# Output stage of a three-part kernel: first two units in halves side by side, p's raw places exchanged, conversions in a set order

## The chip, the cores and the metric

The kernel runs on 1 core of one Trainium2 chip. The metric is the time of one execution in microseconds (us) of device time; of several runs the median counts. Lower is better.

## The reference

What is computed is a decayed causal attention and two feed-forward blocks behind it, all in float32:

```python
scores = scale * q @ k.T + (cum_i - cum_j), causal;  attn = softmax(scores);  x = attn @ v      # 4 batches, 8 heads, 576 x 64
h = x @ w_in;   g = max(0.01 * h, h);   x = g @ w_out         # 2304 tokens, 512 -> 2048 -> 512
a = x @ w_a;    b = x @ w_b;            out = (a * b) @ w_out2 # 2304 tokens, 512 -> 1536 -> 512
```

Only the last line is touched by the change, and of it the product with `w_out2` and the end of the two products before it.

## The kernel before

TensorE multiplies in a rounded float32 form. Each operand is split into a rounded part and the rest of it (high and low, function `parts`, L933 on ScalarE for the high part and L934 on VectorE for the low part), and each product is made in three passes (high x high, high x low, low x high). The matrices of the second feed-forward block are multiplied by a seven-product scheme on 2 x 2 blocks, so an operand of four blocks is first turned into seven (`seven_of_four`, L955 to L959): four blocks as they are, then three sums of them (L957 and L958 on VectorE), each set then split by `parts`.

**Third layer** (`l3_unit`, matmuls L1090). `a` and `b` are made for 6 pairs of 128-column blocks (i = 0 to 5), for token blocks u = 0 and u = 1 of 1024 tokens and a last one. `b`'s unit ends with the multiplication by `a` (L1103) and `p_store` (L1074 to L1076): two additions on VectorE and a store of p to DRAM. The very last of these, of i = 5 and u = 1, is put off (`held["store"]`) and called where the caller wants it.

**Fourth layer** (`l4_unit`, matmuls L1200). There are 9 units n of 2 x 128 tokens. A unit multiplies p by the six row blocks of `w_out2` (j = 0 to 5), 7 products of 3 passes for each j, 126 matmuls of 256 columns in all, into four banks of PSUM, and then adds the products up (L1207 to L1221) and stores the output rows. p comes back from DRAM in halves: half h = 0 holds j = 0 to 2 and half h = 1 holds j = 3 to 5 (`load_p`, DMA at L1172; `convert_p` makes the seven split blocks of a half). The weights come as four plus three blocks from DRAM (`load_o2`, DMA at L1149) and are split by `convert_o2`.

**Places.** SBUF is full, so raw and split operands land in places that the third layer has just done with. Raw p(0,1), the second half of unit 0, lands in a place that the third layer's operands for u = 0 leave; p(0,0) has a place of its own; p(1,0), p(1,1) and the later halves take turns in the four tiles of the third layer named o0, o1, a0, a1. Raw weight block 3 lands in two small tiles that are also used for other things (`words`); blocks 4 and 5 land in places that the third layer's operands for u = 1 leave.

**Order.** The kernel is written as a program order, and a scheduler decides the order of the instructions of each engine from it. The program before calls, between the steps of the third layer's last block (i = 5): after the first step the load and split of weight block 0, and the load of p(0,0); after the third step weight block 1; after the fourth step what is left of `later`, the load of p(0,1), the splits of p(0,0), weight block 2 and p(0,1), and the loads of weight block 3, p(1,0) and p(1,1). Then, behind the third layer, weight blocks 3 to 5, p(1,0) and p(1,1) are split, the put-off store is called, and the units follow one after the other, each with the loads and the split of unit n + 2 around it:

```python
    for n in range(NB1):
        if n + 2 < NB1:
            for h in range(2):
                load_p(n + 2, h)
        l4_unit(n)
```

Of the kernel before, what the change touches and what calls it, by code (L numbers as in the profile page):

```python
# [26 lines left out]
def kernel(  # L27
# [903 lines left out]

    def parts(hi, lo, src):
        nc.scalar.copy(hi, src)  # L933
        nc.vector.tensor_tensor(out=lo, in0=src, in1=f32(hi), op=ALU.subtract)  # L934
# [18 lines left out]
    def seven_of_four(w, t, op):  # L953

        parts(w(0)[:, 0:4], w(1)[:, 0:4], t)  # L955
        second = t[:, 1:2]
        nc.vector.tensor_tensor(out=t[:, 2:4], in0=t[:, 2:4], in1=second.to_broadcast([P, 2, *t.shape[2:]]), op=ALU.subtract)  # L957
        nc.vector.tensor_tensor(out=t[:, 1], in0=t[:, 1], in1=t[:, 0], op=op)  # L958
        parts(w(0)[:, 4:7], w(1)[:, 4:7], t[:, 1:4])  # L959

# [111 lines left out]
    def p_store(o, i, t0, n):  # L1072

        nc.vector.tensor_tensor(out=o[:, 1], in0=o[:, 1], in1=o[:, 3], op=ALU.add)  # L1074
        nc.vector.tensor_tensor(out=o[:, 1], in0=o[:, 1], in1=o[:, 0], op=ALU.subtract)
        nc.sync.dma_start(p_dram[i // 3, :, i % 3, :, t0 : t0 + n].rearrange("b p t -> p b t"), o)  # L1076

    def l3_unit(i, z, u):
# [22 lines left out]
        def store():  # L1101
            if z:
                nc.vector.tensor_tensor(out=o[:, 1:4], in0=o[:, 1:4], in1=at[:, 1:4], op=ALU.mult)  # L1103
                p_store(o, i, 512 * u, 512)

        def last():
            if (i, z, u) == (NP - 1, 1, 1):
                held["store"] = store
            else:
                store()  # L1110
# [40 lines left out]
    def convert_o2(i):  # L1151
        if i == 0:
            place = pools["ea"].tile([P, SLOT], F32R, tag="a", name=f"w_o2_{i}")
        elif i == 2:
            place = pools["ex"].tile([P, SLOT], F32R, tag="w", name=f"w_o2_{i}")
# [20 lines left out]
    def convert_p(n, h):  # L1176

        if n % 2 == 0 and h:
            x = pools["ex"].tile([P, 5384], F32R, tag="x", name=f"px_{n}")[:, 8:]
        else:  # L1180
            x = rounded(((8, None), (5 * SLOT + 72, 5384))[n % 2][h], 5376)
        x = xps[n, h] = x.rearrange("p (b l i t) -> p b l i t", b=7, l=2, i=3)
        seven_of_four(lambda l: x[:, :, l], raw_p[n, h], ALU.add)
# [3 lines left out]
    def l4_unit(n):  # L1187
# [4 lines left out]
        banks = [bank(f"o_{n}_{z}") for z in range(5 if final else 4)]  # L1192
# [3 lines left out]
        order = [(j, m) for m in PRODUCTS for j in range(NP)] if final else [(j, m) for j in range(NP) for m in PRODUCTS]  # L1196
        for j, m in order:
            z, y = place[m]
            for e, (xl_, wl) in enumerate(PASSES):
                nc.tensor.matmul(  # L1200
                    ps[m], xps[n, j // 3][:, X_ROWS[m], xl_, j % 3, :], wo2[j][:, O_COLS[m], wl, :],
                    start=(j == e == y == 0), stop=(j == NP - 1 and e == 2 and y == ends[z]),
                )
        o = words(F32, f"o_{n}").rearrange("p (b n) -> p b n", b=4)
# [127 lines left out]
    def y_pool():  # L1332
        e_ctx.close()
        pools["ey"] = e_ctx.enter_context(tc.tile_pool(name="ey", bufs=1))
# [32 lines left out]
    for i in range(NP):  # L1367
# [5 lines left out]
        for s, (z, u) in enumerate(steps):  # L1373
# [21 lines left out]
            if i == NP - 1:  # L1395
                if s == 0:
                    load_o2(0)
                    load_p(0, 0)
                    convert_o2(0)
                    load_o2(2)  # L1400
                if s == 2:
                    load_o2(1)
                    convert_o2(1)
                if s == 3:
                    while later:
                        later.pop(0)()
                    e_ctx.close()
                    pools["ex"] = e_ctx.enter_context(tc.tile_pool(name="ex", bufs=1))
# [12 lines left out]
    for h in range(2):  # L1421
        convert_p(1, h)
    held["store"]()
    for n in range(NB1):
# [3 lines left out]
        l4_unit(n)  # L1428
        if n + 2 < NB1:
            for h in range(2):  # L1430
                convert_p(n + 2, h)
# [30 lines left out]
```

## Time and profile before

| | |
|---|---|
| median of 3 runs | 1033.9 us (1032.48 to 1035.31) |
| the profiled execution, its time | 1030.66 us |
| its span, first to last instruction | 1028.9 us |
| TensorE busy | 1005.5 us (98%) |
| VectorE, ScalarE busy | 671.6 us (65%), 557.9 us (54%) |
| mean granted clock of TensorE | 0.992 |

The profile gives, for one execution, the busy time of each engine, the chain of work that ended last, the instructions in order of time, and for each wait what ended it. TensorE is busy nearly all the time, so a change can only win where TensorE stands still or runs at the lower clock. The fourth layer begins at about 877 us from the span's start.

### The profile page before, as it was taken

How to read it: one execution, taken by the hardware profiler on the slowest of the kernel's cores; microseconds unless marked ns; L12 is line 12 of the kernel's file. 1: busy time of each engine (PE TensorE's matmuls, PEld its weight loads, DVE VectorE, ACT ScalarE, POOL GpSimd, SP SyncE). 2: the span in 40 equal slices, each digit the busy share in tenths (PEclk: the TensorE clock that was granted, in tenths of full speed). 3: DMA queues.
4: the chain of work that ended last, by engine and by line, in shares of the span. 5: the costliest groups of instructions: out<-in, count | busy, mean ns of one | idle time of the engine just before them, and what ended most of it. 6: DMA issues, size and time to landing. Idle time of an engine off the chain costs nothing.

```text
span 1028.9 us, 19822 instructions
## 1 busy us (share of the span) xinstructions
PE 1005.5 (98%) x7299; PEld 913.8 (89%) x7299; DVE 671.6 (65%) x1383; ACT 557.9 (54%) x1144; POOL 178.4 (17%) x402
## 2 busy tenths in 40 slices
PE   6899999999999999999999999999999999899998
PEld 5677779999999999999999997888888888799998
DVE  5799656755626555264367547668686675898872
ACT  6688687986748867488455444232322222354430
POOL 3525325442413324133000000000000000000000
PEclk9899999999999999999999999999999999999999
DMA  8997145543532436321583123233151423757711
GB/s 218 270 266 217 48 96 110 106 93 62 112 78 62 92 62 110 80 55 45 188 298 119 62 62 103 94 122 118 57 164 41 159 100 125 238 150 203 212 53 42
DMA packets 230497, 125.78 MB, mean 122 GB/s; under 512 B 144704, under 2 KB 212160, under 8 KB 230400
## 3 DMA queue, kind: packets, MB, share of 16 engines
q1 hardware_dynamic: 224784, 118.67, 42.0%
q10 hardware_dynamic: 5616, 5.84, 1.7%
q8 instruction: 58, 0.95, 0.4%
q14 instruction: 39, 0.32, 0.1%
HBM read 95.29 MB, written 29.17 MB: 121 GB/s over the span
## 4 chain that ended last, share of the span: by engine, by line
PE 92%; DMA 4%; ACT 1%; DVE 1%; POOL 1%; issue 1%; SPq 0%; ACTq 0%; POOLq 0%; DVEq 0%
PE h L865 19%; PE y L895 19%; PE o L1200 12%; PE s L99 6%; PE b_b L1090 5%; PE b_a L1090 5%; PE av L99 5%; PE pp L99 4%; PE a_a L1090 3%; PE a_b L1090 3%; PE d_b L1090 3%; PE d_a L1090 3%; DMA homef<-in_moe_w_out_dram 2%; PE a_last L1122 2%; PE b_last L1122 2%; DMA homef<-o_dram 1%
## 5 line engine op out<-in xcount | busy, mean ns | idle before, releaser
L895 PE MATMUL y<-gh,homer 128*128 128x256 f32 x1152 | 227.2, 284 | 0.6 <-ACT gh L877 0.6
L865 PE MATMUL h<-xh,homer 128*128 128x256 f32 x1152 | 225.6, 283 | 0.9 <-ACT hs L878 0.9
L865 PEld LDWEIGHTS h<-xh,homer 128*128 128x128 f32 x1152 | 183.4, 188 | 5.6 <-issue 2.7
L895 PEld LDWEIGHTS y<-gh,homer 128*128 128x128 f32 x1152 | 183.8, 188 | 3.8 <-issue 2.1
L895 PE MATMUL y<-gl,homer 128*128 128x256 f32 x576 | 162.5, 284 | 0.0
L865 PE MATMUL h<-xl,homer 128*128 128x256 f32 x576 | 161.6, 281 | 0.0
L895 PEld LDWEIGHTS y<-gl,homer 128*128 128x128 f32 x576 | 108.4, 188 | 1.1 <-issue 0.9
L865 PEld LDWEIGHTS h<-xl,homer 128*128 128x128 f32 x576 | 108.3, 188 | 0.5
L390 POOL TENSOR_SCALAR p<-cumb,ncum_t 128x384 f32<-128x384 f32 (+2 forms) x112 | 75.7, 679 | 149.3 <-PE pp L99 86.3
L880 DVE TENSOR_TENSOR gl<-hs,gh 128x512 fp32r<-128x512 f32 x72 | 50.9, 707 | 71.9 <-ACT hs L878 71.3
L373 ACT ACTIVATE p<-p,stat 128x256 f32<-128x256 f32 (+3 forms) x123 | 73.6, 600 | 36.0 <-DVE stat L402 30.7
L402 DVE CUSTOM_DVE_ANT_0 p<-s,p 128x384 f32<-128x384 f32 (+2 forms) x100 | 48.4, 491 | 39.6 <-PE s L99 29.8
L877 ACT ACTIVATE gh<-h 128x512 fp32r<-128x512 f32 x72 | 42.7, 593 | 41.7 <-PE h L865 40.9
L411 ACT ACTIVATE p<-p,rec 128x384 f32<-128x384 f32 (+1 forms) x108 | 56.1, 572 | 11.5 <-DVE rec L379 10.6
L99 PE MATMUL pp<-ident,p 128*128 128x128 f32 (+1 forms) x376 | 62.2, 276 | 0.0
L1200 PE MATMUL o<-homer,homer 128*128 128x256 f32 x441 | 57.7, 284 | 0.0
L1200 PEld LDWEIGHTS o<-homer,homer 128*128 128x128 f32 x441 | 55.2, 191 | 0.2
L1200 PE MATMUL o<-w_o,homer 128*128 128x256 f32 x378 | 52.6, 284 | 1.4 <-ACT homer L933 1.4
L933 ACT CAST homer<-p 128x1536 fp32r<-128x1536 f32 (+1 forms) x26 | 33.7, 1320 | 35.3 <-DVE p L958 20.4
L1200 PEld LDWEIGHTS o<-w_o,homer 128*128 128x128 f32 x378 | 48.6, 191 | 2.1 <-ACT homer L933 1.8
L99 PEld LDWEIGHTS pp<-ident,p 128*128 128x128 f32 (+1 forms) x376 | 43.4, 139 | 4.0 <-issue 2.3
L99 PE MATMUL av<-pt,vn 128*64 128x320 f32 (+4 forms) x400 | 46.9, 372 | 0.0
(272 smaller groups left out, 2047.6 us busy)
## 6 DMA issues: line engine op xcount, KB each, us to landing
p<-p_dram SPq DMA_DIRECT2D x17, 768.0 KB, 6.6
p_dram<-p SPq DMA_DIRECT2D x12, 1024.0 KB, 4.3
cumb<-cum_dram SPq DMA_DIRECT2D x32, 288.0 KB, 3.9
homef<-in_moe_w_out_dram SPq DMA_DIRECT2D x15, 511.6 KB, 6.0
homef<-in_moe_w_in_dram SPq DMA_DIRECT2D x15, 510.5 KB, 4.7
raw_o<-in_moe_w_out_dram SPq DMA_DIRECT2D x12, 511.6 KB, 5.9
xq<-in_q_dram SPq DMA_DIRECT2D x144, 32.0 KB, 2.1
y_dram<-yo ACTq DMA_DIRECT2D x18, 256.0 KB, 2.9
```

The costliest lines, as they stand in the source:

```text
L99: return method(*args, **kw)
L373: act_att.activation(pt, pt, AF.Exp, bias=stat[:, 0, s : s + 1], scale=-1.0, accum_out=stat[:, 1, s : s + 1])
L390: made = pool_att.tensor_scalar(pt, cumb[:, :n], 1.0, ncum_t[:, t, bh : bh + 1], op0=ALU.mult, op1=ALU.add)
L402: dve_att.tensor_tensor_reduce(out=pt, in0=sp[:, :n], in1=pt, op0=ALU.add, op1=ALU.min, scale=1.0, scalar=ABOVE, accum_out=stat[:, 0, s : ...
L411: act_att.mul(ps[i], ps[i], rec[:, i : i + 1])
L865: made = nc.tensor.matmul(hps[:, u, :], w[:, c * P : c * P + P], x[:, c, :], start=(n == 0), stop=(n == 3 * ND - 1))
L877: nc.scalar.activation(gh, hps, AF.Prelu, alpha=0.01)
L880: nc.vector.tensor_tensor(out=gl, in0=hs, in1=f32(gh), op=ALU.subtract)
L895: nc.tensor.matmul(o, w[:, d * P : d * P + P], g[:, u, :], start=(fi == 0 and n == 0 and d % 2 == 0), stop=(fi == NF1 - 1 and n == 2 and d ...
L1090: nc.tensor.matmul(to, w[:, W_ROWS[m], wl, c2 * P : c2 * P + P], y[c2][xl_][:, Y_COLS[m], :], start=(first and c2 == e == 0), stop=(c2 == ...
L1122: nc.tensor.matmul(ps[:, f * T1 : f * T1 + T1], w[:, wb, wl, c2 * P : c2 * P + P], y[:, xb, xl_, c2 * T1 : c2 * T1 + T1], start=(f == m == ...
L1200: nc.tensor.matmul(ps[m], xps[n, j // 3][:, X_ROWS[m], xl_, j % 3, :], wo2[j][:, O_COLS[m], wl, :], start=(j == e == y == 0), stop=(j == N ...
```

## The change

Five edits, all around the start of the fourth layer:

- `l4_unit(n, h)` can do one half of a unit alone. Units 0 and 1 are now done as: first half of 0, first half of 1, second half of 0, second half of 1. All other units are as before.
- The raw places are exchanged: p(1,0) now lands where p(0,1) landed (the place left by u = 0), p(0,1) in o1, p(1,1) in a0, and the later halves take the four tiles in another rotation. The places of the split halves are exchanged in the same way.
- Raw weight block 3 lands in one piece of 1792 columns in a place that the third layer's last `a` weights leave, in place of the two small tiles; its split is then one instruction of each kind and not two.
- `seven_of_four` and `convert_o2` are made into generators, and `by_turns` names the order in which their pieces are called; `next_in` then adds an order dependence between each such instruction and the one before it on the same engine (ScalarE, VectorE), from the fourth step of i = 5 to the split of p(2,1). The put-off multiplication L1103 and store come between these pieces: the multiplication between weight blocks 4 and 5, the additions and the store within the split of unit 2.
- The split of unit 2 is called before the second half of unit 1.

```diff
+    border = {}
+
+    def next_in(engine, made):
+        if border:
+            if border.get(engine) is not None:
+                tc.add_manual_dep(made.ins, border[engine].ins.name, ORDER, reason="order between the stages")
+            border[engine] = made
+
     def parts(hi, lo, src):
-        nc.scalar.copy(hi, src)
-        nc.vector.tensor_tensor(out=lo, in0=src, in1=f32(hi), op=ALU.subtract)
+        next_in("act", nc.scalar.copy(hi, src))
+        next_in("dve", nc.vector.tensor_tensor(out=lo, in0=src, in1=f32(hi), op=ALU.subtract))
...
+        elif i == 3:
+            raw_o2[i] = [(plain(2 * SLOT, 7 * T1).rearrange("p (b n) -> p b n", b=7), 0, 7)]
...
+    def by_turns(turns, **of):
+        for name in turns.split():
+            next(of[name])
...
-        if (n, h) == (0, 1):
+        if (n, h) == (1, 0):
             src = plain(5392, 1536).rearrange("p (b i t) -> p b i t", b=4, i=3)
         else:
-            pool, tag = ("r", ("o1", "a0", "a1", "o0")[(2 * n + h - 2) % 4]) if n else ("ey", "s")
+            tag = {(0, 0): "s", (0, 1): "o1", (1, 1): "a0"}.get((n, h)) or ("a1", "o1", "a0", "o0")[(2 * n + h) % 4]
+            pool = "r" if n or h else "es"
...
-        if n % 2 == 0 and h:
-            x = pools["ex"].tile([P, 5384], F32R, tag="x", name=f"px_{n}")[:, 8:]
+        if n % 2 and h == 0:
+            x = pools["ex"].tile([P, 5440], F32R, tag="x", name=f"px_{n}")[:, 8:5384]
         else:
-            x = rounded(((8, None), (5 * SLOT + 72, 5384))[n % 2][h], 5376)
+            x = rounded(((8, 5 * SLOT + 72), (None, 5384))[n % 2][h], 5376)
...
-        order = [(j, m) for m in PRODUCTS for j in range(NP)] if final else [(j, m) for j in range(NP) for m in PRODUCTS]
+        js = range(NP) if h is None else range(3 * h, 3 * h + 3)
+        order = [(j, m) for m in PRODUCTS for j in js] if final else [(j, m) for j in js for m in PRODUCTS]
...
+                    load_p(1, 0)
+                    by_turns("a a b a b w b w", a=convert_p(0, 0), b=convert_p(1, 0), w=convert_o2(2))
                     load_p(0, 1)
-                    convert_p(0, 0)
-                    convert_o2(2)
-                    convert_p(0, 1)
-                    load_o2(3)
-                    load_p(1, 0)
-                    load_p(1, 1)
     later.pop(0)()
-    for j in range(4, NP):
+    for j in range(3, NP):
         load_o2(j)
-    for j in range(3, NP):
-        convert_o2(j)
-    for h in range(2):
-        convert_p(1, h)
-    held["store"]()
-    for n in range(NB1):
+    load_p(1, 1)
+    l4_unit(0, 0)
+    l4_unit(1, 0)
+    late_x = convert_p(1, 1)
+    by_turns(
+        "x x u x v s y w y y", x=convert_p(0, 1), y=late_x, s=held["store"], u=convert_o2(3), v=convert_o2(4), w=convert_o2(5)
+    )
+    l4_unit(0, 1)
+    for h in range(2):
+        load_p(2, h)
+    more = [convert_p(2, h) for h in range(2)]
+    by_turns("a a", a=more[0])
+    all_of(held["store"])
+    by_turns("a b b b", a=more[0], b=more[1])
+    border.clear()
+    for n in range(1, NB1):
...
-        l4_unit(n)
+        l4_unit(n, 1 if n < 2 else None)
```

On each engine the order of the instructions is the same up to these places, and the counts of matmuls are equal.

SyncE issues the DMAs. In its rows below, `p_dram<-p_0` is the store of p for i = 5, u = 0, the last that half 1 of the units 0 to 3 needs; `homef_1536` is the raw place left by u = 0, `p_0` and `p_1` on the left of an arrow are halves 0 and 1 of a unit, `t_o_3`, `homef_1792` and `homef_3584` are raw weight blocks. Before:

```order
L1076 DMA p_dram<-p_0_10896 128x4x512
L1172 DMA homef_1536_10964<-p_dram 128x12x128
L1172 DMA p_0_10989<-p_dram 128x12x128
L1172 DMA p_1_10991<-p_dram 128x12x128
L1149 DMA t_o_3_0_10985<-o_dram 128x1024
L1149 DMA homef_3584_11099<-o_dram 128x7x256
L1149 DMA t_o_3_4_10986<-o_dram 128x768
L1149 DMA homef_3584_11101<-o_dram 128x7x256
L1172 DMA p_0_11131<-p_dram 128x12x128
L1076 DMA p_dram<-p_1_11039 128x4x512
```

With the change, from the same place:

```order
L1196 DMA homef_1536_10971<-p_dram 128x12x128
L1092 DMA p_dram<-p_0_10899 128x4x512
L1167 DMA homef_1792_11100<-o_dram 128x1792
L1196 DMA p_1_10992<-p_dram 128x12x128
L1196 DMA p_1_11106<-p_dram 128x12x128
L1167 DMA homef_3584_11102<-o_dram 128x7x256
L1167 DMA homef_3584_11104<-o_dram 128x7x256
```

and, right behind these:

```order
L1196 DMA p_1_11338<-p_dram 128x12x128
L1196 DMA p_0_11336<-p_dram 128x12x128
L1196 DMA p_0_11355<-p_dram 128x12x128
L1255 DMA out_dram<-o_11328 128x512 x2
L1255 DMA out_dram<-o_11422 128x512
L1092 DMA p_dram<-p_1_11040 128x4x512
L1255 DMA out_dram<-o_11422 128x512
L1196 DMA p_0_11443<-p_dram 128x12x128
L1196 DMA p_1_11357<-p_dram 128x12x128
```

The load into `homef_1536`, now p(1,0), has moved ahead of the store; raw weight block 3 is one load and has moved ahead of p(0,1) and p(1,1); the loads of unit 2 (with one of unit 3, `p_0_11355`) stand behind all weights; the store of i = 5, u = 1 (`p_dram<-p_1`) has moved from behind one load of unit 2 to behind three loads of units 2 and 3 and three stores of output.

VectorE at the end of the third layer, from the last addition of `b` for u = 0 on (`a_1`, `p_1` belong to u = 1, `p_0` with a 768 or 384 wide row to the sums of p(0,0), `homer_5376` to its split). Before:

```order
L989 TENSOR_TENSOR p_0_10896<-b_b_0_10898,p_0_10896 128x512
L1103 TENSOR_TENSOR p_0_10896<-p_0_10896,a_0_10762 128x1536
L934 TENSOR_TENSOR homer_5376_10966<-p_0_10823,homer_5376_10966 128x4x384
L983 TENSOR_TENSOR a_1_10993<-b_a_1_10995,a_1_10993 128x512
L1074 TENSOR_TENSOR p_0_10896<-p_0_10896 128x512
L985 TENSOR_TENSOR a_1_10993<-d_a_1_10996,a_1_10993 128x512
L957 TENSOR_TENSOR p_0_10823<-p_0_10823 128x768
L977 TENSOR_TENSOR p_1_11039<-b_b_1_11041,p_1_11039 128x512
L1075 TENSOR_TENSOR p_0_10896<-p_0_10896 128x512
```

With the change:

```order
L1005 TENSOR_TENSOR p_0_10899<-b_b_0_10901,p_0_10899 128x512
L1119 TENSOR_TENSOR p_0_10899<-p_0_10899,a_0_10765 128x1536
L999 TENSOR_TENSOR a_1_10994<-b_a_1_10996,a_1_10994 128x512
L1090 TENSOR_TENSOR p_0_10899<-p_0_10899 128x512
L1001 TENSOR_TENSOR a_1_10994<-d_a_1_10997,a_1_10994 128x512
L1091 TENSOR_TENSOR p_0_10899<-p_0_10899 128x512
L947 TENSOR_TENSOR homer_5376_10973<-p_0_10826,homer_5376_10973 128x4x384
L993 TENSOR_TENSOR p_1_11040<-b_b_1_11042,p_1_11040 128x512
L995 TENSOR_TENSOR p_1_11040<-d_b_1_11043,p_1_11040 128x512
```

The two additions ahead of the store (L1074 and L1075, now L1090 and L1091) stand ahead of the split of p(0,0); the second was the eighth row behind the first row shown, and is now the fifth.

TensorE where the first half of unit 0 ends (`o_0_11135` to `o_3_11138` are unit 0's banks and `o_3_11293` is unit 1's; the operand on the right of a comma is the split p, `px_10978` p(0,1); `homer_3584_9374` is weight block 3). Before:

```order
L1200 MATMUL o_3_11138<-w_o_2_10973,homer_5376_10966 128x256 x2
L1200 MATMUL o_0_11135<-w_o_2_10973,homer_5376_10966 128x256 x5
L1200 MATMUL o_1_11136<-w_o_2_10973,homer_5376_10966 128x256 x5
L1200 MATMUL o_2_11137<-w_o_2_10973,homer_5376_10966 128x256 x5
L1200 MATMUL o_3_11293<-w_o_0_10825,homer_5376_11113 128x256 x2
L1200 MATMUL o_0_11290<-w_o_0_10825,homer_5376_11113 128x256 x2
L1200 MATMUL o_3_11138<-homer_3584_9374,px_10978 128x256
L1200 MATMUL o_0_11135<-homer_3584_9374,px_10978 128x256
L1200 MATMUL o_3_11293<-w_o_0_10825,homer_5376_11113 128x256
L1200 MATMUL o_0_11290<-w_o_0_10825,homer_5376_11113 128x256 x4
```

With the change (`o_0_11108` to `o_3_11111` are unit 0's, `o_0_11175` to `o_2_11177` unit 1's, `px_10974` is p(1,0), `homer_5376_11243` p(0,1), `homer_3584_9377` weight block 3):

```order
L1229 MATMUL o_1_11176<-homer_3584_10896,px_10974 128x256 x6
L1229 MATMUL o_2_11177<-homer_3584_10896,px_10974 128x256 x6
L1229 MATMUL o_0_11175<-w_o_2_10985,px_10974 128x256 x5
L1229 MATMUL o_1_11176<-w_o_2_10985,px_10974 128x256 x6
L1229 MATMUL o_2_11177<-w_o_2_10985,px_10974 128x256 x6
L1229 MATMUL o_3_11111<-homer_3584_9377,homer_5376_11243 128x256
L1229 MATMUL o_0_11108<-homer_3584_9377,homer_5376_11243 128x256
L1229 MATMUL o_1_11109<-homer_3584_9377,homer_5376_11243 128x256
L1229 MATMUL o_2_11110<-homer_3584_9377,homer_5376_11243 128x256
L1229 MATMUL o_3_11111<-homer_3584_9377,homer_5376_11243 128x256 x2
L1229 MATMUL o_0_11108<-homer_3584_9377,homer_5376_11243 128x256 x5
```

Before, the first matmuls on weight block 3 and p(0,1) stand behind the 63 matmuls of unit 0's first half and 4 of unit 1's; with the change they stand behind all 126 of both first halves.

## Rows read from the trace of the kernel before

**Rows 1.** The chain that ended last, from 850 us: start us, us, what

```profile
882.05 1.37 PE b_b L1090 x6
...
891.76 9.37 DMA homef<-o_dram
...
901.15 2.76 ACT homer L933 x2
...
903.95 121.22 PE o L1200 x1022
```

**Rows 2.** Busy time by stretch: us, busy PE, PEld, DVE, ACT, POOL, PE clock, DMA, GB/s

```profile
876.97:888.31 11.34, 11.34 (x69) 10.04 (x68) 9.33 (x13) 3.05 (x4) 0.00 (x0) 1.00 0.55 183
888.31:903.95 15.64, 11.30 (x77) 10.50 (x76) 15.07 (x15) 10.12 (x8) 0.00 (x0) 0.89 1.13 336
903.95:1025.17 121.22, 121.20 (x1022) 121.00 (x1022) 89.20 (x98) 41.80 (x39) 0.00 (x0) 1.00 0.44 129
```

**Rows 3.** TensorE in order of time: start us, us, instructions, idle before and releaser

```profile
876.97 0.52 PE L1200 MATMUL o<-w_o,homer 128*128 128x256 f32 x3
...
886.76 1.55 PE L1090 MATMUL b_b<-homer,homer 128*128 128x512 f32 x6
...
892.48 0.74 PE L1200 MATMUL o<-w_o,homer 128*128 128x256 f32 x4 [0.98 <-ACT homer L933]
895.97 0.51 PE L1200 MATMUL o<-homer,px 128*128 128x256 f32 x2 [2.76 <-ACT homer L933]
...
902.90 0.62 PE L1200 MATMUL o<-homer,px 128*128 128x256 f32 x3 [0.17 <-ACT homer L933]
903.95 0.74 PE L1200 MATMUL o<-w_o,homer 128*128 128x256 f32 x4 [0.43 <-ACT homer L933]
```

**Rows 4.** Busy time by stretch, one microsecond after the standstill

```profile
897.00:898.00 1.00, 1.00 (x6) 1.00 (x6) 1.00 (x2) 0.51 (x1) 0.00 (x0) 0.50 1.00 373
```

**Rows 5.** SyncE, DMA issues in order of time

```profile
879.32 0.36 SPq L1076 DMA_DIRECT2D p_dram<-p  x1
883.50 0.36 SPq L1172 DMA_DIRECT2D homef<-p_dram  x1
...
896.28 3.26 SPq L1076 DMA_DIRECT2D p_dram<-p  x1
```

**Rows 6.** ScalarE in order of time

```profile
871.27 1.48 ACT L933 CAST homer<-p 128x1536 fp32r<-128x1536 f32 x1 [1.68 <-PE b_b L1090]
...
888.20 1.48 ACT L933 CAST px<-homef 128x1536 fp32r<-128x1536 f32 x1 [3.28 <-DMA homef<-p_dram]
...
897.49 1.69 ACT L933 CAST homer<-homef 128x1792 fp32r<-128x1792 f32 x1 [1.57 <-DMA homef<-o_dram]
...
899.82 1.15 ACT L933 CAST px<-homef 128x1152 fp32r<-128x1152 f32 x1
...
907.81 0.37 ACT L1207 COPY o<-o 128x256 f32<-128x256 f32 x1
```

**Rows 7.** VectorE in order of time

```profile
872.00 1.76 DVE L1103 TENSOR_TENSOR p<-p,a 128x1536 f32<-128x1536 f32 x1
873.67 1.75 DVE L934 TENSOR_TENSOR homer<-p,homer 128x1536 fp32r<-128x1536 f32 x1
...
878.61 0.68 DVE L1075 TENSOR_TENSOR p<-p 128x512 f32<-128x512 f32 x1
...
881.76 1.35 DVE L934 TENSOR_TENSOR homer<-p,homer 128x1152 fp32r<-128x1152 f32 x1
...
894.69 0.95 DVE L957 TENSOR_TENSOR homef<-homef 128x768 f32<-128x768 f32 x1
...
898.17 0.55 DVE L958 TENSOR_TENSOR homef<-homef 128x384 f32<-128x384 f32 x1
899.21 2.03 DVE L934 TENSOR_TENSOR homer<-homef,homer 128x1792 fp32r<-128x1792 f32 x1 [0.49 <-ACT homer L933]
...
910.30 0.68 DVE L1208 TENSOR_TENSOR o<-o,o 128x512 f32<-128x512 f32 x1
```

More of the change, by code (lines that the diff above doesn't have):

```diff
@@ L955, in seven_of_four @@
         parts(w(0)[:, 0:4], w(1)[:, 0:4], t)
-        second = t[:, 1:2]
-        nc.vector.tensor_tensor(out=t[:, 2:4], in0=t[:, 2:4], in1=second.to_broadcast([P, 2, *t.shape[2:]]), op=ALU.subtract)
-        nc.vector.tensor_tensor(out=t[:, 1], in0=t[:, 1], in1=t[:, 0], op=op)
+        yield
+        second = t[:, 1:2].to_broadcast([P, 2, *t.shape[2:]])
+        next_in("dve", nc.vector.tensor_tensor(out=t[:, 2:4], in0=t[:, 2:4], in1=second, op=ALU.subtract))
+        next_in("dve", nc.vector.tensor_tensor(out=t[:, 1], in0=t[:, 1], in1=t[:, 0], op=op))
+        yield
         parts(w(0)[:, 4:7], w(1)[:, 4:7], t[:, 1:4])
+        yield
     def words(kind, name):
@@ L1072, in p_store @@
     def p_store(o, i, t0, n):
-        nc.vector.tensor_tensor(out=o[:, 1], in0=o[:, 1], in1=o[:, 3], op=ALU.add)
-        nc.vector.tensor_tensor(out=o[:, 1], in0=o[:, 1], in1=o[:, 0], op=ALU.subtract)
+        next_in("dve", nc.vector.tensor_tensor(out=o[:, 1], in0=o[:, 1], in1=o[:, 3], op=ALU.add))
+        next_in("dve", nc.vector.tensor_tensor(out=o[:, 1], in0=o[:, 1], in1=o[:, 0], op=ALU.subtract))
         nc.sync.dma_start(p_dram[i // 3, :, i % 3, :, t0 : t0 + n].rearrange("b p t -> p b t"), o)
@@ L1102, in store @@
             if z:
-                nc.vector.tensor_tensor(out=o[:, 1:4], in0=o[:, 1:4], in1=at[:, 1:4], op=ALU.mult)
+                next_in("dve", nc.vector.tensor_tensor(out=o[:, 1:4], in0=o[:, 1:4], in1=at[:, 1:4], op=ALU.mult))
+                yield
                 p_store(o, i, 512 * u, 512)
         def last():
[L1107 to L1110, printed above, removed]
+            held["store"] = store()
+            if (i, z, u) != (NP - 1, 1, 1):
+                all_of(held["store"])
         three_banks(f"{'ab'[z]}_{i}_{u}", [o[:, q] for q in range(4)], 512, product, first, last)
@@ L1154, in convert_o2 @@
         elif i == 2:
-            place = pools["ex"].tile([P, SLOT], F32R, tag="w", name=f"w_o2_{i}")
+            place = pools["ew"].tile([P, SLOT], F32R, tag="w", name=f"w_o2_{i}")
         else:
@@ L1191, in l4_unit @@
         final = n == NB1 - 1
-        banks = [bank(f"o_{n}_{z}") for z in range(5 if final else 4)]
+        if n not in outs:
+            outs[n] = [bank(f"o_{n}_{z}") for z in range(5 if final else 4)]
+        banks = outs[n]
         place = {1: (3, 0), 2: (0, 0), 6: (0, 1), 5: (1, 0), 7: (1, 1), 3: (2, 0), 4: (4, 0) if final else (2, 1)}
@@ L1202, in l4_unit @@
                     start=(j == e == y == 0), stop=(j == NP - 1 and e == 2 and y == ends[z]),
+                    skip_group_check=h is not None,
                 )
+        if h == 0:
+            return
         o = words(F32, f"o_{n}").rearrange("p (b n) -> p b n", b=4)
@@ L1333, in y_pool @@
         e_ctx.close()
-        pools["ey"] = e_ctx.enter_context(tc.tile_pool(name="ey", bufs=1))
+        for name in ("ey", "es"):
+            pools[name] = e_ctx.enter_context(tc.tile_pool(name=name, bufs=1))
     LEAD = 2
@@ L1402 @@
                     load_o2(1)
-                    convert_o2(1)
+                    all_of(convert_o2(1))
                 if s == 3:
+                    border.update(act=None, dve=None)
                     while later:
```

18 lines of the change are left out of this document (13 added, 5 removed).

## The prediction

> **What bounds the kernel now.** I looked first for the time in which TensorE is not at its best, since it is busy 98% of the span. The chain that ended last [rows 1] is matmuls almost throughout; near its end it leaves TensorE for one stretch, through a weight transfer of 9.37 us and two ScalarE casts, and comes back at 903.95. From there 1022 matmuls of the fourth layer take 121.22 us, 0.1186 us each. Nothing stands still in those, so that is the price of one. The stretches [rows 2] say what the gap is worth: from 888.31 to 903.95 TensorE ran 77 matmuls, which at 0.1186 are 9.1 us, in 15.64 us: **6.5 us lost**. The same row shows why: transfers at 336 GB/s with the DMA engines full, and VectorE busy 15.07 of 15.64 us. TensorE in order of time [rows 3] gives the waits: 0.98, 2.76, 0.17 and 0.43 us, 4.3 in all, each ended by a ScalarE cast. The other 2.2 us are the clock: after that low activity the granted clock fell to its lower level, half, as in the microsecond from 897 [rows 4], in which 6 matmuls ran and not 8. Ahead of 888.31 TensorE is busy 11.34 of 11.34 us, and behind 903.95 121.20 of 121.22 [rows 2]. So the change can win 6.5 us at most, in this place alone.
>
> What TensorE waits for there is, by the order of its matmuls, p(1,0) (0.98 and 0.43) and the second half of unit 0, weight block 3 and p(0,1) (2.76 and 0.17). The store of p for i = 5, u = 0 goes out at 879.32, the load of p(0,1) behind it at 883.50 [rows 5], its cast starts at 888.20 [rows 6]; the weights come behind it in full queues. Only 67 matmuls can run meanwhile.
>
> **The work on TensorE does not change**: same matmuls, same widths, only their order. The third layer's last 30 matmuls of 512 columns, in sixes at 1.37 us [rows 1], are 6.8 us; the 126 of both first halves at 0.1186 are 14.9. Begun at 876.97 [rows 3] as before, they reach to 898.7, where before TensorE had nothing ready after about 891.5. So the question is whether all operands are there in time.
>
> *First halves.* p(1,0) no longer needs the late store. Its place is free with the last product of u = 0, at about 871 (the cast at 871.27 waits for the same product [rows 6]). A load like it took 4.7 us, 883.50 to 888.20 [rows 5, 6], so it lands at about 876, in a stretch without transfers, and TensorE asks for it at 885. Covered by 9 us less a cast of 1.48.
>
> *The store* needs a multiplication (from 872.00) and two additions ahead of which the order now has only two others: 872.00 + 1.67 + 4 x 0.6 = 876.1, against 878.61 + 0.68 before [rows 7]. It gains 3 us. With 4.2 us (879.32 to 883.50) p(0,1) can be asked for at 880.4. With weight block 3, now one transfer into a place free at about 880, and p(1,1), 2.4 MB are then under way, 7.2 us at 336 GB/s, down by 888. Blocks 4 and 5 follow when the third layer's u = 1 operands are done, at about 887.5 and 888.3 (its last product starts at 886.76 and takes 1.55 [rows 3]), and are there by 895. The transfers do not bind any more.
>
> *VectorE* has nothing to spare, so I add it up. Back to back an instruction starts 0.08 before the end of the one ahead (873.67 behind 872.00 + 1.76), so by [rows 7] a 512-wide one takes 0.60, a 1536-wide one 1.67, 1152 1.27, 768 0.87, 384 0.47, 1792 1.95; a 1024-wide one, between 768 and 1152, 1.14. From 872.00 to the low part of weight block 3 the new order has 11 of 512, 4 of 1536, 4 of 768, 3 of 384, 2 of 1152, one of 1024, one of 1792: 6.6 + 6.7 + 3.5 + 1.4 + 2.5 + 1.1 + 1.95 = 23.8, so 895.8. TensorE asks at 899.2: 3.4 spare. Then low parts of p(0,1)'s sums, weight block 4, the put-off multiplication, p(1,1) and weight block 5 at 897.1, 899.0, 900.7, 902.4 and 904.3; TensorE asks for the four operands at 900.5, 902.2, 904.7 and 906.6. At least 2.2 spare. ScalarE's casts (1.48, 1.69, 1.15 [rows 6]) run ahead of these. The put-off multiplication stood ahead of all this before; its 1.67 us are in the sum.
>
> *What is late next* is unit 2. Unit 0 now ends late, at about 908.6. Its output copy (0.37 [rows 6]) waits for TensorE until 907 and stands on ScalarE ahead of the casts of p(1,1)'s sums and p(2,0), which end at 908.5 and 909.9, where TensorE asks for them at 909.4 and 909.9. Then p(3,0): its place is that of raw p(1,1), read last at 910.0; 4.7 us of load and 1.48 of cast make 916.2, and behind it in ScalarE's order stand the casts of p(2,0)'s sums (917.3) and p(2,1) (918.8). TensorE asks for the first at 916.9 and, after 8 matmuls, for the second: a standstill of 0.4 and one of 0.5. I take **1.0 us**. From below it is nothing (a quicker load); from above, with a load as slow as the 9.37 us of [rows 1], 5.7. I take the short load since it is nearest: one transfer in a quiet stretch. Neither wait is longer than the first of 0.98, so I leave the clock at its upper level.
>
> From there VectorE has two splits a unit, 2 x (1.67 + 0.87 + 0.47 + 1.27) = 8.6, and 4 output additions, 2.4, under 14.9 of TensorE, as before.
>
> Merging weight block 3's split (1024 and 768 into 1792) saves 0.06 us, nothing on the path. **Sum**: 6.5 - 1.0 = 5.5. The profiled execution, 1030.66 with a span of 1028.9, becomes 1025.2. The median stands 3.2 above that execution: 1033.9 - 5.5 = **1028.4 us**.
>
> **The rivals.** *The place at 905 to 919 costs more.* The casts and sums arrive with no slack there, and ScalarE serves in a set order, so the late p(3,0) holds p(2,0) and p(2,1), which have long landed. With a load of 7 us rather than 4.7 and small delays the gain is 1.5 to 4, the time 1030 to 1032.4, about half of it within 0.3%. For it: VectorE is full to 912. Chance 0.14.
>
> *Banks.* Two open units hold all eight banks up to 908.6, so unit 2 begins in a bank of unit 0, which must be emptied by a copy of 0.37 and four additions of at most 0.68 that stand among the splits [rows 6, 7]. If none of that were hidden it would cost 2.5 us more: 1030.9. Against it: unit 1 has 32 matmuls, 3.8 us, in between. Chance 0.05. The Trainium skill (Perfetto Trace Analysis, Matmuls) speaks for this rival: independent matmul groups should rotate through the banks, so that emptying one overlaps the next group's matmuls; two units ending together rotate less. The trace of before shows no such order.
>
> *The wait only moves.* If p(0,1) or weight block 3 were split 3.4 us later than worked out, TensorE would stand between the halves, with a microsecond more for each; at 4.3 us of that and the lower clock behind it all 6.5 are gone: 1033.9. That needs 7.7 us, where I find the transfers done 0.3 us ahead of their places. Chance 0.07.
>
> *Slower.* The store of i = 5, u = 1, issued at 896.28 before [rows 5], now stands in SyncE's order behind three loads that wait for places and three stores of output: by VectorE's order at about 919. p(3,1), whose place it empties, waits for it, and p(5,0) and p(4,1) wait behind in the queue. With 4.2 for the store and 4.7 to 9.37 for the load it lands at 928 to 932; TensorE asks for it at about 937. If it were down only after 942, 6.4 us of standstill and 2.2 of clock would make 8.6, 3.1 more than is won: 1037. Chance 0.04.
>
> **How the numbers follow.** What a measurement here can tell from no change is about 0.3%, 3.1 us: 1030.8. My forecast, with standstills between 0 and 2.5 us, 1027.4 to 1029.9, has 0.70. Faster: 0.70, half of the first rival and of the second, 0.09: 0.79. Same: the other half and the moved wait, 0.09 + 0.07, and 0.01 for rounding: 0.17. Slower: 0.04. The lower end is the full 6.5 with the 1.4 us by which the runs of before scatter about their median, 1026.0; the upper end takes in most of the first two rivals, 1032.0.
>
> **What would show it.** In the changed profile: the store of u = 0 at about 876 and p(1,0)'s load ahead of it; TensorE without a wait from 877 to 909 and at full clock at 897; any waits at 915 to 920, ended by ScalarE; the last matmul ending about 5.5 us before 1025.17. I am wrong if a wait of over 1 us stands at 898 to 903 (the moved wait), if waits at 905 to 920 sum to over 3, or if a unit from the fourth on waits for p.

## The result, and the profile after

The changed kernel took **1025.6 us** (median of 6 runs, 1024.01 to 1028.24), beside 1034.9 of the kernel before (6 runs, 1032.48 to 1036.8): a ratio of 0.9913, with a 95% interval of 0.9892 to 0.9933, or 9.0 us less (the medians differ by 9.3). Forecast were 1028.4 us, 5.5 less, in a range from 1026.0 to 1032.0. Sign and place were right; the time lies 0.4 us under the range.

The profiled execution took 1024.01 us, with a span of 1022.2 and a mean granted clock of 0.995. Its fourth layer begins at 875.60, where that of before began at 876.97 [rows 3]. In the rows of the changed kernel L946 is the high part on ScalarE (L933 before), L947 the low part on VectorE (L934), L1229 the matmuls of the fourth layer (L1200), and L1239 to L1253 add up and copy its output. The same three stretches as [rows 2], counted from there:

```profile
875.60:886.94 11.34, 11.34 (x69) 10.08 (x68) 11.18 (x14) 3.67 (x4) 0.00 (x0) 1.00 0.95 289
886.94:902.58 15.64, 15.64 (x134) 15.64 (x133) 15.54 (x13) 9.59 (x8) 0.00 (x0) 1.00 0.71 205
902.58:1018.96 116.38, 115.00 (x966) 114.28 (x964) 86.30 (x98) 39.84 (x38) 0.00 (x0) 1.00 0.47 135
```

In the second, 134 matmuls ran where 77 had, without a wait and at full clock, and the transfers fell from 336 to 205 GB/s: the first row shows where they went, into the stretch ahead (289 where 183 had been). The third has 1.38 us in which TensorE stood. TensorE in order of time, the answer to [rows 3]:

```profile
875.60 0.52 PE L1229 MATMUL o<-w_o,homer 128*128 128x256 f32 x3
...
917.08 0.74 PE L1229 MATMUL o<-w_o,homer 128*128 128x256 f32 x4 [1.21 <-ACT homer L946]
...
918.47 0.75 PE L1229 MATMUL o<-homer,homer 128*128 128x256 f32 x4 [0.17 <-ACT homer L946]
...
1017.74 1.22 PE L1229 MATMUL o<-homer,homer 128*128 128x256 f32 x9
```

The chain that ended last, the answer to [rows 1], leaves the matmuls in this layer only there, through two output additions and a low part on VectorE, the load of p(3,0), whose place that low part frees, and three casts:

```profile
887.03 19.18 PE o L1229 x162
...
909.08 5.40 DMA p<-p_dram
914.48 0.02 issue
914.50 1.48 ACT px L946
915.98 2.44 ACT homer L946 x2
918.42 0.04 issue
918.47 100.51 PE o L1229 x847
```

SyncE, the answer to [rows 5], shows p(1,0)'s load ahead of the store, and the store 4.5 us earlier than at 879.32, 1.4 of them the earlier start:

```profile
869.66 0.36 SPq L1196 DMA_DIRECT2D homef<-p_dram  x1
874.80 0.36 SPq L1092 DMA_DIRECT2D p_dram<-p  x1
878.66 0.33 SPq L1167 DMA_DIRECT2D homef<-o_dram  x1
879.10 1.30 SPq L1196 DMA_DIRECT2D p<-p_dram  x2
886.36 1.25 SPq L1167 DMA_DIRECT2D homef<-o_dram  x2
```

From the start of the first matmul of the fourth layer to the end of the last, the **stage** took 148.2 us before (876.97 to 1025.15) and 143.4 after (875.60 to 1018.96): 4.8 us. Two things were open: why the times differ by more than the stage, and which part of the change carries the gain.

### The profile page after: what moved, and what is told of

The parts are those of the page before. It is cut to its first block, busy times and chain, and to the rows that moved or that the text cites. A ratio compares the mean times of both kernels' runs of the same rounds, so it can differ in the third digit from the quotient of the medians.

```text
span 1022.2 us, 19811 instructions
## 1 busy us (share of the span) xinstructions
PE 1001.3 (98%) x7299; PEld 910.8 (89%) x7299; DVE 669.8 (66%) x1382; ACT 556.5 (54%) x1143; POOL 179.5 (18%) x402
## 4 chain that ended last, share of the span: by engine, by line
PE 89%; DMA 5%; ACT 2%; issue 2%; POOL 1%; DVE 1%; SPq 0%; ACTq 0%; POOLq 0%; DVEq 0%
PE y L895 19%; PE h L865 18%; PE o L1229 12%; PE s L99 5%; PE b_b L1106 5%; PE b_a L1106 5%; PE av L99 4%; PE pp L99 4%; PE a_a L1106 3%; PE a_b L1106 3%; PE d_b L1106 3%; PE d_a L1106 3%; DMA cumb<-cum_dram 2%; PE a_last L1138 2%; PE b_last L1138 2%
## 5 line engine op out<-in xcount | busy, mean ns | idle before, releaser
L390 POOL TENSOR_SCALAR p<-cumb,ncum_t 128x384 f32<-128x384 f32 (+2 forms) x112 | 73.7, 662 | 147.9 <-PE pp L99 93.5
L1229 PE MATMUL o<-homer,homer 128*128 128x256 f32 x672 | 85.3, 281 | 0.2 <-ACT homer L946 0.2
L1229 PEld LDWEIGHTS o<-homer,homer 128*128 128x128 f32 x672 | 81.9, 188 | 0.5 <-ACT homer L946 0.4
L946 ACT CAST homer<-p 128x1536 fp32r<-128x1536 f32 (+1 forms) x28 | 36.5, 1319 | 32.4 <-DVE p L972 19.9
L947 DVE TENSOR_TENSOR homer<-p,homer 128x1536 fp32r<-128x1536 f32 (+1 forms) x28 | 43.3, 1551 | 6.3 <-ACT homer L946 6.3
L99 PE MATMUL s<-ks,qhh 128*128 128x288 f32 (+4 forms) x144 | 44.3, 315 | 1.5 <-DVE stat L113 0.8
## 6 DMA issues: line engine op xcount, KB each, us to landing
p_dram<-p SPq DMA_DIRECT2D x12, 1024.0 KB, 4.3
```

What stands on the lines that cost most here:

```text
L99: return method(*args, **kw)
L390: made = pool_att.tensor_scalar(pt, cumb[:, :n], 1.0, ncum_t[:, t, bh : bh + 1], op0=ALU.mult, op1=ALU.add)
L947: next_in("dve", nc.vector.tensor_tensor(out=lo, in0=src, in1=f32(hi), op=ALU.subtract))
L1229: nc.tensor.matmul(ps[m], xps[n, j // 3][:, X_ROWS[m], xl_, j % 3, :], wo2[j][:, O_COLS[m], wl, :], start=(j == e == y == 0), stop=(j == N ...
```

## The experiments: the two kernels again

Two theories of the surplus: the loss of before at 888 to 904 varies from execution to execution, or the surplus lies ahead of the stage, in layers that the change doesn't touch. Both kernels were run again, unchanged.

> The kernel before, unchanged, for a second profiled execution. In the first, the stage from the first matmul of the fourth layer to the last lasted 148.2 us (876.97 to 1025.17), with 4.3 us of waits and some 2 us of half clock at 888 to 904; the kernel after needed 143.4 us (875.60 to 1018.98). The trace pair explains 4.8 us there, the medians differ by 9.3. Theory 1 (the loss at 888 to 904 varies with when the loads land, and the first profile caught a small one): the stage lasts 149.5 to 152 us here, with 6 to 9 us lost at 888 to 904, and the stage begins at 876 to 877.5. Theory 2 (the rest lies ahead of the stage, in layers that the change doesn't touch): the stage lasts 148.0 to 148.6 us again and begins at 878 or later.

> The changed kernel, unchanged, for a second profiled execution. Theory 1: the stage lasts 143.0 to 144.0 us again, begins within 0.5 us of where the kernel before begins it on this chip, and the kernel is 8 to 10 us faster than before. Theory 2: the stage lasts 143.4 us as well, but begins 3 us or more ahead of that of the kernel before.

> The changed kernel unchanged, for a third sample of its time: the first two gave 9.0 and 5.7 us below before, while the stages of the profiled executions differ by 4.8 to 5.3 us. Theory (the part of 9.0 above that is scatter ahead of the fourth layer, in the first 130 us of the program): the stage lasts 143.0 to 143.4 us and the time is 4 to 7 us below before. Rival (the change also gains ahead of the fourth layer): 8 us or more below before again.

Timed beside before on the same chip, the changed kernel gave ratios of 0.9945 (0.9923 to 0.9967) and 0.9937 (0.9911 to 0.9963), by these ratios 5.7 us under 1032.95 and 6.5 under 1032.78. The stages were 148.3 for before and 143.0 and 143.2 for the changed kernel, the start of before came at 879.42: the second theory's numbers. Whether that start is always late, or scatters, three more executions of before and one of the changed kernel tell.

> The kernel before again, for its stage lengths alone. Two executions gave 148.2 and 148.3 us from the first matmul of the fourth layer to the end of the last, three of the changed kernel 143.0 to 143.4, that is 5.1 us between them, while all timed runs so far put the means 6.5 us apart, give or take 1.0. Theory (the stage of before is the same in every execution, and what is above 5.1 us is scatter ahead of it): 147.9 to 148.6 us here, and a start between 874 and 881. Rival (the stage of before is longer in some executions, by the loads that fill its queues): 149 us or more here or in one of the next two.

> As for the third execution of before: 147.9 to 148.6 us by the theory, 149 us or more in at least one of the three by the rival.

> As for the third execution of before: 147.9 to 148.6 us by the theory, 149 us or more in at least one of the three by the rival.

> The changed kernel again: by both theories 143.0 to 143.4 us from the first matmul of the fourth layer to the end of the last, with 1.0 to 1.4 us of waits at 917 to 919.

| execution | time, us | start of the stage | stage |
|---|---|---|---|
| before, first to fifth | 1030.7, 1033.2, 1035.0, 1027.3, 1038.2 | 876.97, 879.42, 881.54, 873.71, 884.37 | 148.2, 148.3, 147.9, 148.1, 148.2 |
| changed, first to fourth | 1024.0, 1023.8, 1025.4, 1023.9 | 875.60, 875.60, 877.11, 875.61 | 143.4, 143.0, 143.2, 143.2 |

The stage is the same in every execution within 0.4 us; the start moves by 10.7 us in the kernel before alone. So the first theory falls, and the second holds in this form: **the surplus lies ahead of the stage, where the time scatters**. Where it scatters shows in the slowest and the quickest execution of before. TensorE's longest wait in the slowest:

```profile
66.79 0.79 PE L895 MATMUL y<-gh,homer 128*128 128x256 f32 x2 [3.41 <-ACT gh L877]
```

and the stretches around it. Within that standstill, from 63.4 to 66.8, the granted clock fell to half (1.2 GHz), and it stayed there until 79, for 13 us; in the quickest execution it is 1.00 from 58 to 82:

```profile
64.00:68.00 4.00, 1.21 (x5) 1.21 (x6) 3.75 (x10) 4.00 (x9) 0.00 (x0) 0.74 0.67 176
68.00:72.00 4.00, 4.00 (x19) 3.34 (x17) 3.46 (x6) 3.00 (x5) 0.93 (x1) 0.50 0.98 333
72.00:79.00 7.00, 7.00 (x26) 5.26 (x26) 4.33 (x9) 3.57 (x6) 0.29 (x1) 0.50 0.64 182
```

The cast that TensorE waits for stands on ScalarE behind a conversion of weights whose load is late, in the slowest execution by 3.87 us:

```profile
62.79 1.12 ACT L147 ACTIVATE c_a<-homef 128x1024 f32<-128x1024 int8 x1 [3.87 <-DMA homef<-in_moe_w_out_dram]
```

In the quickest it is late by 1.45, and TensorE waits for no cast of this kind until 75:

```profile
58.35 1.15 ACT L147 ACTIVATE c_a<-homef 128x1024 f32<-128x1024 int8 x1 [1.45 <-DMA homef<-in_moe_w_out_dram]
```

In the slowest that load is issued at 56.42 and lands at 62.68, in the quickest it is issued at 53.50 and lands at 58.24; what makes it late is not shown. Compared instruction by instruction on TensorE, the slowest execution is level with the quickest at 57 us (0.1 us ahead), 9.4 us behind it at 74, and 10.7 behind at the first matmul of the fourth layer. So the wait and the half clock behind it make most of this difference.

Of the 17 profiled executions of this study, five have a wait of TensorE for this cast of 2.7 to 3.4 us, and their stage begins at 879.4 to 884.4; twelve have none above 1.6, and it begins at 873.7 to 878.6. The changed kernel draws from the same lot: its order of instructions on every engine is that of before up to the third layer's last iteration, and kernels made from it below began the stage anywhere from 874.52 to 880.28. Over all runs the mean of before is 1033.14 us (111 runs, 1027.7 to 1040.0), that of the changed kernel 1026.66 (27 runs, 1023.8 to 1032.9): 6.5 us, give or take 1.0. The stages give 4.9. What is left, 1.5, is of the size of the scatter: median less stage is 885.0 for before and 883.3 for the changed kernel, and 882.6 to 885.5 for the eight kernels below. That it is chance and nothing else is not shown.

## The experiments: the parts of the change

With a stage that repeats within 0.4 us, one profile tells parts apart that times don't. Each part was undone by itself.

**The raw places as before.**

```diff
-        if (n, h) == (1, 0):
+        if (n, h) == (0, 1):
...
-            tag = {(0, 0): "s", (0, 1): "o1", (1, 1): "a0"}
+            tag = {(0, 0): "s", (1, 0): "o1", (1, 1): "a0"}
```

> The changed kernel with one part undone: the raw landing places of p(0,1) and p(1,0) are again those of before; halves, block 3's place and the set order stay. Theory (the exchange of the places carries the gain, since only it lets p(1,0) land before the fourth layer begins): p(1,0)'s load waits for the store of the first part of p and lands at 884 or later, and what stands behind its cast in ScalarE's order comes late too; TensorE waits 4 to 7 us between 880 and 900, and the time is 4 to 7 us over the changed kernel. Rival (the set order alone carries it, places are indifferent): within 0.5 us of the changed kernel.

Stage 148.8 (875.99 to 1024.80), that is 5.6 over the changed kernel; time 1031.4 us, ratio to before 0.9999 (0.9976 to 1.0023). The theory holds. The chain names the load as foretold; it lands at 886.39:

```profile
879.49 6.90 DMA p<-p_dram
886.39 0.02 issue
886.41 1.47 ACT px L946
887.88 1.06 ACT homer L946
888.94 0.04 issue
888.99 23.21 PE o L1229 x181
```

TensorE waited 3.82 us for it, where 4 to 7 were foretold, and the clock came down behind (0.83 from 885 to 895).

**No set order.**

```diff
-                    border.update(act=None, dve=None)
```

> The changed kernel without the set order of the conversions on ScalarE and VectorE; halves, raw places and block 3's place stay. Theory (the exchanged places carry the gain, the order only keeps conversions that aren't due yet from going ahead): the store of p's second half comes later and p(0,1) lands late, the stage lasts 144 to 147.5 us, that is 1 to 4 us over the changed kernel, with a wait on p(0,1)'s conversion at 890 to 900. Rival (the order carries it): 148 us or more. Rival (the order is idle): 143 us.

Stage 148.0 (875.29 to 1023.34), 4.8 over; time 1032.5, ratio 0.9994 (0.9968 to 1.0019). By its size that is the first rival's number, 148 or more; the theory said 147.5 at most, and the order carries more than it allowed. How it carries it is the theory's chain: the late store. VectorE makes the store's second addition at 878.60, 4.5 us later than in the changed kernel, so SyncE issues the store at 879.90 and p(0,1)'s load, behind the next block's, at 888.05, where the changed kernel had 879.10:

```profile
879.47 0.33 SPq L1167 DMA_DIRECT2D homef<-o_dram  x1
879.90 0.38 SPq L1092 DMA_DIRECT2D p_dram<-p  x1
886.45 0.54 SPq L1167 DMA_DIRECT2D homef<-o_dram  x1
888.05 0.36 SPq L1196 DMA_DIRECT2D p<-p_dram  x1
```

p(0,1) lands at 895.0 and p(1,1) at 901.6, where the changed kernel had 886.1 and 888.7. TensorE waits 4.3 us in all; the longest wait is for the cast of p(1,1), and the one behind it for the copy that empties a bank (L1239), which stands on ScalarE behind another cast:

```profile
903.22 1.56 PE L1229 MATMUL o<-homer,homer 128*128 128x256 f32 x11 [2.04 <-ACT homer L946]
906.05 0.80 PE L1229 MATMUL o<-w_o,homer 128*128 128x256 f32 x2 [1.26 <-ACT o L1239]
```

**Weight block 3 in the small tiles.**

```diff
-        elif i == 3:
-            raw_o2[i] = [(plain(2 * SLOT, 7 * T1).rearrange("p (b n) -> p b n", b=7), 0, 7)]
```

(and its two turns in the list of turns)

> The changed kernel with block 3 of the output weights landing in the two small tiles again, as before; halves, raw places and set order stay. Theory (block 3 is needed first at 897 and has 2 us to spare): its load can start only when block 2's raw tiles are read, near 890, and lands near 895, so its low part is through near 899 and everything behind it in the set order comes 3 to 5 us later: the stage lasts 145 to 148 us. Rival (the place is idle, since blocks 4 and 5 or p(0,1) are as late anyway): within 0.5 us of 143.2.

Stage 146.9 (878.28 to 1025.20), 3.7 over, as the theory has it; time 1031.1, ratio 0.998 (0.9954 to 1.0006). Block 3 is loaded only behind blocks 4 and 5, from 890.39, and ScalarE stands at its cast until it has landed. Four waits of 0.57 to 0.76 follow one another, the first ended by that cast, the other three by VectorE's low parts, which the late cast delays (L1227 is L1229 here):

```profile
899.75 1.78 ACT L946 CAST homer<-t_o 128x1024 fp32r<-128x1024 f32 x2 [7.86 <-DMA t_o<-o_dram]
...
900.85 0.50 PE L1227 MATMUL o<-homer,homer 128*128 128x256 f32 x2 [0.61 <-ACT homer L946]
902.11 1.56 PE L1227 MATMUL o<-homer,homer 128*128 128x256 f32 x11 [0.76 <-DVE homer L947]
904.25 4.80 PE L1227 MATMUL o<-homer,homer 128*128 128x256 f32 x37 [0.57 <-DVE homer L947]
909.63 5.52 PE L1227 MATMUL o<-homer,homer 128*128 128x256 f32 x44 [0.59 <-DVE homer L947]
```

**Units 0 and 1 written whole.**

```diff
-    l4_unit(0, 0)
-    l4_unit(1, 0)
...
-    l4_unit(0, 1)
+    l4_unit(0)
...
-        l4_unit(n, 1 if n < 2 else None)
+        l4_unit(n)
```

> The changed kernel with the first two units written whole, one after the other, as before; raw places, block 3's place and the set order stay. The measure is the stage, from the first matmul of the fourth layer to the end of the last: 143.0 to 143.4 us in two executions of the changed kernel, 148.2 and 148.3 in two of before. Theory (the halves matter little, since the order in which the matmuls stand is nearly the same without them and the operands are there early): 143 to 144 us. Rival (only the halves let TensorE go on while p(0,1) and blocks 3 to 5 are got ready): 146 us or more, with a wait at 885 to 897.

Stage 143.2 (876.77 to 1019.92), as with the halves; time 1026.5, ratio 0.9937 (0.9914 to 0.996). The scheduler interleaves the two units by itself: the order of instructions is the same as with the halves on ScalarE, VectorE and SyncE, and on TensorE six matmuls stand elsewhere. The halves, the first thing that the change names, carry nothing.

**The exchange alone**, with the halves, block 3's landing and the set order undone. What stays of the change beside it is the order in which the program calls the conversions, with unit 2's split ahead of the end of unit 1.

> The kernel before with one part of the change alone: the raw places of p(0,1) and p(1,0) are exchanged and p(1,0) is loaded early; whole units, block 3 in the small tiles, no set order. With each of three parts undone by itself, the stage lasted 148.8 (places as before), 148.0 (no set order) and 146.9 us (block 3 as before) against 143.2 us of the changed kernel and 148.2 of before. Theory (the three parts are links of one chain, each worth nothing without the others): 147 to 150 us. Rival (the parts add up, and the exchange is the largest of them): 144 us or less.

Stage 149.8 (880.28 to 1030.05), longer than before; time 1033.5, ratio 0.9993 (0.9968 to 1.0017). p(1,0) comes early, but the store only at 884.29. Block 3 is cast last, behind block 5, for whose load ScalarE stood 2.44 us; TensorE waits first for that cast and then for its low part on VectorE:

```profile
902.90 1.69 ACT L946 CAST homer<-homef 128x1792 fp32r<-128x1792 f32 x1 [2.44 <-DMA homef<-o_dram]
904.50 1.77 ACT L946 CAST homer<-t_o 128x1024 fp32r<-128x1024 f32 x2
...
905.59 0.74 PE L1227 MATMUL o<-homer,homer 128*128 128x256 f32 x4 [3.32 <-ACT homer L946]
908.43 1.86 PE L1227 MATMUL o<-homer,homer 128*128 128x256 f32 x7 [2.11 <-DVE homer L947]
```

So places, order and block 3's landing are **links of one chain**: undone singly they take back 5.6, 4.8 and 3.7 of 4.9 us, and the exchange without the other two brings nothing. The last of the five edits, unit 2's split called early, was never undone, so what it is worth is not shown.

## The experiments: the new standstill

**The set order kept longer**, through the split of unit 3, so that p(3,0) stands behind p(2,1)'s sums:

```diff
-    border.clear()
     for n in range(1, NB1):
...
+        if n == 1:
+            border.clear()
```

> The changed kernel with the set order kept until the casts of p(2,0) and p(2,1) are through, so that ScalarE no longer stands with the cast of p(3,0)'s sums, whose load waits for a place, ahead of the casts that TensorE needs. Theory (the 1.4 us standstill of TensorE at 917 to 919 hangs on that one order): the waits at 917 go, the stage lasts 142.0 us in place of 143.4, and the time is 1.0 to 1.6 us under that of the changed kernel, 10 to 11 us under before. Rival (p(2,1) is short of time by itself, or p(3,0) is then late): the wait turns up within 10 us later, and the time is within 0.4 us of the changed kernel.

Stage 144.8 (880.21 to 1025.04), so 1.6 longer; time 1030.3, ratio 0.9973 (0.9952 to 0.9994). The standstill shrinks to 0.45, but p(3,0) is cast behind p(2,1)'s sums, at 926.61, which counted from the stage's start is 7.5 us later than in the changed kernel (12 by the time in the trace, as the next expectation has it). So its own sums are cast late too, and they meet the next late load: ScalarE stands for 4.86 us at the cast of p(4,1), whose load waited for the place of p(2,1), and casts p(3,0)'s sums behind it. TensorE waits 2.04 us for them. That is the rival in kind, but it comes 17 us behind the first standstill, not within 10, and costs 1.6 us:

```profile
935.94 1.47 ACT L946 CAST homer<-p 128x1536 fp32r<-128x1536 f32 x1 [4.86 <-DMA p<-p_dram]
937.32 1.15 ACT L946 CAST px<-p 128x1152 fp32r<-128x1152 f32 x1
...
938.52 0.73 PE L1229 MATMUL o<-w_o,px 128*128 128x256 f32 x4 [2.04 <-ACT px L946]
```

**p(3,0) behind p(2,1)'s cast only.**

```diff
-    by_turns("a b b b", a=more[0], b=more[1])
+    by_turns("a b", a=more[0], b=more[1])
+    last_cast = border["act"]
     border.clear()
+    all_of(more[1])
...
+                if (n, h) == (1, 0):
+                    border["act"] = last_cast
+                    next(p)
...
```

> The changed kernel with one dependence more: ScalarE casts p(3,0)'s raw parts only behind the casts of p(2,0)'s sums and of p(2,1); the set order ends before p(2,1)'s additions, unlike the kernel that kept it to the end and lost 1.6 us in the stage by casting p(3,0) 12 us later. Theory (TensorE's standstill at 917 hangs on ScalarE holding the cast of p(3,0) ahead of the others until its load has landed): that standstill goes, p(3,0) is cast 2 to 3 us later than in the changed kernel, and the stage lasts 141.8 to 142.6 us in place of 143.0 to 143.4. Rival (p(3,0) has no 3 us to spare): a wait on px or on p(3,0)'s sums of 1 us or more at 920 to 945, and the stage lasts 143 us or more.

Stage 144.3 (878.61 to 1022.92); time 1028.6, ratio 0.9957 (0.9935 to 0.9978). The rival's stage, by a way that neither had: 0.46 is left of the standstill, and ScalarE now takes p(4,0) ahead of p(2,1)'s sums and stands at its load:

```profile
928.70 2.53 ACT L946 CAST homer<-p 128x1536 fp32r<-128x1536 f32 x2 [7.56 <-DMA p<-p_dram]
```

TensorE waits 0.67 and 0.58 us behind it.

**ScalarE's order set anew**: p(2,1), p(2,0)'s sums, p(3,0), p(2,1)'s sums, p(4,0).

```diff
-    by_turns("a b b b", a=more[0], b=more[1])
-    border.clear()
+    by_turns("b a b", a=more[0], b=more[1])
+    last = {1: border["act"]}; border.clear(); border["act"] = None; all_of(more[1]); last[2] = border["act"]; border.clear()
...
+                if n < 3 and h == 0:
+                    border["act"] = last[n]; next(p); border.clear()
...
```

(and p(2,1)'s cast and its low part are two turns in place of one)

> The changed kernel with ScalarE's order set anew around the standstill at 917: p(2,1)'s raw parts are cast ahead of p(2,0)'s sums (their load landed near 904, ScalarE is idle from 908.7 to 914.5), p(3,0) behind those sums, p(4,0) behind p(2,1)'s sums. Theory (the two standstills, 1.0 to 1.4 us, hang only on ScalarE standing at p(3,0) till its load lands, and the kernel that put p(3,0) behind p(2,1)'s cast lost its gain to p(4,0) standing ahead of p(2,1)'s sums): p(2,0)'s sums are cast near 914.2 in place of 915.9, the wait at 917 is under 0.3 us, none of 0.5 us follows, and the stage lasts 142.0 to 142.5 us in place of 143.0 to 143.4; the time is 0.6 to 1.4 us under that of the changed kernel. Rival (VectorE, which makes the low parts, is what p(2,0)'s sums and p(2,1) wait for): a wait of 0.7 us or more stays at 916 to 919, now on VectorE, and the stage lasts 143 us or more.

Stage 142.1 (874.52 to 1016.58), with no wait of TensorE in the whole fourth layer. p(2,0)'s sums are cast at 913.14, as soon as VectorE has them, in an execution whose stage begins 1.08 us ahead of that of the first changed one (L966 is the cast of raw parts here):

```profile
905.89 2.85 ACT L966 CAST homer<-p 128x1536 fp32r<-128x1536 f32 x2
908.64 0.37 ACT L1239 COPY o<-o 128x256 f32<-128x256 f32 x1
913.14 1.16 ACT L946 CAST homer<-p 128x1152 fp32r<-128x1152 f32 x1 [4.13 <-DVE p L972]
914.21 1.48 ACT L966 CAST px<-p 128x1536 fp32r<-128x1536 f32 x1
```

The theory holds. The time, 1026.7 (11 runs, ratio to before 0.9925, 0.9897 to 0.9953), stands beside 1027.2 of the changed kernel on the same chip; the stage shows the 1.1 us, the times can't.

## Why the prediction was right, and where it was wrong

**The loss and its cover: right.** The stage without a wait is 142.1 (the last kernel), that of before 148.1 in the mean of five: 6.1 us of loss, where "6.5 us lost" was read from the matmul count, 0.4 too many.

**Operands in time: right.** In the changed profile the store went out at 874.80 (876.1 less the 1.37 by which the stage began earlier: 874.7). The low part of weight block 3 ended at 895.1, worked out at 894.4. Unit 0's copy started at 905.64, worked out at 905.6. No wait stands at 898 to 903. The transfers were a little slower than worked out: p(1,1) landed at 888.7 and block 5 at 894.4, where 888 and 895 less 1.37 make 886.6 and 893.6. One sum was short: two halves of p and block 3 are 2.5 MB, 7.4 us at 336 GB/s, not 2.4 and 7.2. Nothing waited for either.

**The halves: a wrong reason.** "The 126 of both first halves" reach as far as I said, but TensorE's order has them so without the halves, as the whole units show.

**The new standstill: right.** Foretold were 0.4 and 0.5, **1.0 us** taken; four executions show 1.0 to 1.4, by the stages 143.2 - 142.1 = 1.1. The two parts were sized wrong, 0.9 to 1.2 and 0.2 for 0.4 and 0.5, and the sum came out. The load took 5.40 us, not 4.7. Its mechanism is the one foretold, since a new order on ScalarE alone removes it.

**The rivals.** Waits at 905 to 919 came to no more. No bank was waited for: with two units open at once the changed kernel's trace shows no wait that an emptying copy ended. In the kernel without the set order one does stand, at 906.05, of 1.26 us. The Trainium skill (Perfetto Trace Analysis, Matmuls) asks that independent matmul groups rotate through the banks, so that emptying one overlaps the next group's matmuls. The price set on this rival, 2.5 us, is below its own terms: 0.37 and four of 0.6 are 2.8. The wait didn't move. The store of i = 5, u = 1 went out at 918.40, foretold near 919, and nothing waited for p(3,1).

**The sum: 5.5 forecast, 4.9 by the stages** (148.1 - 143.2, or 6.1 of loss less 1.1 of standstill, each rounded). So the gain in the stage was smaller than forecast, and still the time lies under the range: the mechanism didn't put it there. The step that failed is the last, where the gain becomes a time: "The lower end is the full 6.5 with the 1.4 us by which the runs of before scatter about their median". Three runs showed 1.4; 111 spread from 1027.7 to 1040.0, since the start of the stage moves by 10 us. Six runs of each put the kernels 9.0 us apart, two larger samples 5.7 and 6.5. Against the means over all runs, the six of before stand 1.8 us high and the six of the changed kernel 0.8 low, which is luck. So the term that was mis-sized is the scatter: as an estimate, the 111 runs deviate by 2.9 us about their mean, so a mean of six moves by 2.9 / sqrt(6) = 1.2 us, the base of three runs that I subtracted from by 2.9 / sqrt(3) = 1.7, and the two together by 2.1. Twice that under 1027.4 is 1023.2, where the range ended at 1026.0.

## What to carry to other kernels

Measure a local change by the length of its stage in the profile, from a fixed first instruction to a fixed last one: here it repeats within 0.4 us while the time of a run scatters over 12. Where an engine serves in a set order, ask of each instruction what it waits for and what stands behind it: moving the cast that waited for a load took away one standstill and twice made another, until everything that had landed stood ahead of everything that hadn't. A change of several parts can be one chain; undo each part by itself before you believe that any of them is worth its share.

## What was not expected

The scatter of whole runs comes, for a good part, from one early load. At 58 to 63 us a conversion on ScalarE waits 1.45 us for a weight load in the quickest execution of before and 3.87 in the slowest; there TensorE then waits 3.41 us, and the granted clock stays at 0.50 for 13 us, about four times as long as the wait, though TensorE is busy all the time from 66.8 on. What is lost there is carried, whole, to the end: 9.4 us behind at 74, 10.7 at the fourth layer, and from the first matmul of the third layer to the first of the fourth it is 256.4 us in the quickest execution of before (617.33 to 873.71) as in the first changed one (619.21 to 875.60).
